# Folding w_in by even and odd frequencies in 64-column groups, with row sums made on GpSimd

## The chip, the cores and the metric

The kernel runs on one core of one Trainium2 chip. The metric is the time of one execution on the device in microseconds (us). TensorE (PE; its weight loads are PEld), VectorE (DVE), ScalarE (ACT), GpSimd (POOL) and SyncE (SP, which issues most DMAs) each work through their own queue of instructions in order and wait for one another by semaphores.

## The reference

```python
def _attn_ref(x):                      # x: (8, 3008, 256) float32
    X = np.fft.fft(x, axis=1)
    X = np.fft.fft(X, axis=2)
    return X.real.astype(np.float32)

def _moe_ref(x, w_in, w_out):          # x: (24064, 256), w_in (256, 2048), w_out (2048, 256)
    h = x @ w_in
    g = np.where(h > 0.0, h, np.exp(np.minimum(h, 0.0)) - 1.0)
    return (g @ w_out).astype(np.float32)
```

The weights are float64 in memory. The output of the first function, as 24064 rows of 256, is the input of the second.

## The kernel before

**The mathematics.** The transform over the 256 channels is linear and is followed at once by `w_in`, so the kernel never makes it for the data: it multiplies `w_in` by the cosines and sines of the channels instead. This is the *fold*: `Wc` (cosine part) and `Ws` (sine part), 128 x 2048 each. The transform over the sequence is done for the data, by matrices `MC00`, `MC01`, `MC10`, `MC11` (index: cosine or sine, even or odd frequency), on sums and differences of x: `fold_x` reads four pieces `xl0` to `xl3` of a batch and makes even sums `e0` to `e3` and odd differences `o0` to `o3` over channels c and 256 - c, then sums and differences of those (E0, E2, EO0 to EO3, O0, O2). Channel 128 goes a way of its own (`xe`, `rx`, `Rb`).

**Weights.** `w_in` and `w_out` come in eight chunks of 256 columns or rows each. Each is float64 and is turned into float32 by a class `Chunk`: `load` (SyncE's DMA into a *home*), `fields` (two VectorE operations, L212 and L218, on the words), `power` (three ScalarE operations, L366), `round` (GpSimd adds, `w<-raw,w`) and `scale` (VectorE, L255, then a GpSimd multiplication, `w<-w,pow`). The home of chunk c of `w_in` is the tile `WT0` to `WT3` for c = 0 to 3, a half of `Wc` for 4, and `WT0`, `WT1`, `WT2` for 5, 6, 7; homes are used again by later chunks. `fold_chunk(c)` then multiplies by the constants `CC` into PSUM (`H`), and `put_chunk(c)` copies the result to `Ws` and `Wc` on ScalarE.

**Steps.** The main loop has 376 steps of a period T = 4.8 (a unit close to a microsecond), eight for each tile of 256 sequence frequencies; a step treats 256 of the 2048 hidden columns. In each, TensorE multiplies `Wc` by the ring `Rr` (`mm_P`) and `Ws` by `Ir` (`mm_Q`), VectorE makes `E` (L728, from P, before Q may overwrite) and the two halves of the hidden layer (L738), ScalarE the exponentials, VectorE the ELU (L754), and TensorE multiplies by `w_out` into pA to pD. From the third tile on the second product is a Winograd form with seven blocks instead of eight, for which GpSimd makes sums of the activations (`G<-G`, four of 128 x 256 a step) and, once, of the weights: `sum_weights(i)`, four operations on 128 x 128, writes column i of the four tiles `WT0` to `WT3`, `WT2` first. The first 16 steps use the plain form; step pair 2c and 2c + 1 needs chunk c of `w_out`.

**The order.** There is no planner: `at(t, fn)` puts every piece of work at a time in units of the period, and the pieces are recorded sorted by t and kept in that order on each engine where they are pinned; DMAs, which are not, may be moved by the framework. `fold_chunk(c)` stands at `max(2c - 3, c % 3) * T + 4.7` for c > 1, just before the `mm_P` of a step. `sum_weights(i)` stands at `(11 + 0.7 i) T + 1.0`. `fold_x` of the next batch runs on GpSimd, in halves, spread over the steps.

**Channel 128.** At `12 T + 1.35` `ext_rows(1, gtt, 1)` writes two row pieces `rx` on GpSimd. From them SyncE copies to DRAM, and then 16 DMAs `load_ext` read channel 128 of all batches element by element into the same tile tag; `get_ext` brings it back by partition (`xs`), `fold_ext` on GpSimd adds (`xe`), and `dft_ext` on TensorE uses it in four column groups at `25 T + 4.75`. `dft_ext_0` (matmuls `MC,xd`) did the same for one batch earlier, in two groups with one column each.

Of the kernel before, what the change touches and what calls it, by code (L numbers as in the profile page):

```python
# [9 lines left out]
FP = mybir.dt.float32  # L10
# [5 lines left out]
ALU = mybir.AluOpType  # L16
# [39 lines left out]

def _chan_consts():

    c = np.arange(256)
    d = np.arange(129)  # L60
    cos = np.cos(2.0 * np.pi * ((c[:, None] * d[None, :]) % 256) / 256)
    d = np.arange(1, 128)
    sin = -np.sin(2.0 * np.pi * ((c[:, None] * d[None, :]) % 256) / 256)
    m = np.concatenate([cos[:, :128], sin, cos[:, 128:]], axis=1)
    return np.ascontiguousarray(
        m.reshape(2, 128, 256).transpose(1, 0, 2).reshape(128, 512)
    ).astype(np.float32)


# [9 lines left out]
def kernel(  # L79
# [7 lines left out]
    nc = tc.nc  # L87
# [19 lines left out]
    pin = tc.keep_in_program_order  # L107
# [52 lines left out]
        return L  # L160


    CC = cpool.tile([128, 512], FP, tag="CC")
    w2 = cpool.tile([128, NF * ND], FP, tag="w2")
    Wc = cpool.tile([128, NDFF], FP, tag="Wc")
    Ws = cpool.tile([128, NDFF], FP, tag="Ws")
# [7 lines left out]
    class Chunk:  # L174

        def __init__(self, src, dst, raw, tmp, shared):
            self.src, self.dst, self.home, self.tmp_tag = src, dst, raw, tmp
            self.shared = shared  # L180

        def load(self):
            dst = self.dst()
            if not wide:
                nc.sync.dma_start(out=dst, in_=self.src)
                return
            home = self.home
            if isinstance(home, tuple):
                tag, bufs, size = home
                home = spool.tile([128, size], FP, tag=tag, bufs=bufs, name="raw")  # L190
            words = home[:, 0:1024].bitcast(I32)
            self.raw = words.rearrange("p (n w) -> p n w", w=2)
            n = dst.shape[1]
            nc.sync.dma_start(
                out=words.rearrange("p (a b) -> p a b", a=n), in_=self.src.bitcast(I32)
            )
# [37 lines left out]
        def round(self):  # L234
# [11 lines left out]
                )  # L246
            )

        def scale(self):

            if not wide:
                return
            lo, hi, dst = self.parts()
            pin(
                nc.vector.scalar_tensor_tensor(  # L255
                    out=self.t, in0=hi, scalar=-(2**31), in1=self.t,
                    op0=ALU.bitwise_and, op1=ALU.bitwise_or,
                )
            )
            if self.shared:  # L260
                gtt(dst, dst, self.t.bitcast(FP), ALU.mult)
                return
            pin(
                nc.vector.scalar_tensor_tensor(
                    out=dst, in0=dst, scalar=2.0**-20,
                    in1=self.t.bitcast(FP), op0=ALU.mult, op1=ALU.mult,
                )
            )

    def w1_dst(c):  # L270
        q, half = divmod(c, 2)
        if q not in w1:
# [24 lines left out]
            IN_HOMES[c],  # L297
            IN_TMP[c],
            c > 0,
        )  # L300
        for c in range(8)
    ]
# [4 lines left out]
            OUT_HOMES[c],  # L307
            OUT_TMP[c],
            True,
        )  # L310
        for c in range(8)
    ]
# [39 lines left out]
    def mm(out_, lhsT, rhs, start, stop=True):  # L352
        pin(
            nc.tensor.matmul(  # L354
                out_, lhsT=lhsT, rhs=rhs, start=start, stop=stop, skip_group_check=True
            )
        )
# [4 lines left out]
    def gtt(o, a, b, op):  # L362
        pin(nc.gpsimd.tensor_tensor(out=o, in0=a, in1=b, op=op))  # L363
# [6 lines left out]

    def fold_chunk(c):

        q, half = divmod(c, 2)
        ps = folds[c] = bank("H")
        for n, part in enumerate((128, 0)):
            for h in range(2):
                mm(
                    ps[:, 256 * n : 256 * n + 256],
                    CC[:, h * 256 + part : h * 256 + part + 128],
                    w1[q][:, h, half * 256 : half * 256 + 256],  # L380
                    n == 0 and h == 0,
                    h == 1,
                )

    def put_chunk(c):
        cols = slice(c * 256, (c + 1) * 256)
# [43 lines left out]
        gtt(W[3], W[1], b21, ALU.add)  # L430


    OC = slice(0, 6 * 127)

    def fold_x(L, engine_of, pieces):

        ops = {}

        def op(key, o, a, b, f):
            tt = lambda o, a, b, f: pin(  # L440
                engine_of(key).tensor_tensor(out=o, in0=a, in1=b, op=f)
            )
            n = o.shape[1]
            cuts = [n * i // pieces for i in range(pieces + 1)]
            for i in range(pieces):
                c = slice(cuts[i], cuts[i + 1])
                ops[key, i] = lambda c=c: tt(o[:, c], a[:, c], b[:, c], f)

        E, O = [], []
        for j in range(4):  # L450
            e = spool.tile([128, 6 * 128], FP, tag=f"e{j}", bufs=1, name=f"e{j}")
            o = spool.tile([128, 6 * 127 + 1], FP, tag=f"o{j}", bufs=1, name=f"o{j}")
            ev = e.rearrange("p (m d) -> p m d", d=128)
            ov = o[:, OC].rearrange("p (m d) -> p m d", d=127)
            src = L[j].rearrange("p (m d) -> p m d", d=ND)
            if j in (1, 2):
                src = src[:, ::-1]
            lo, hi = src[:, :, 1:128], src[:, :, 255:128:-1]
            op(f"e{j}", ev[:, :, 1:128], lo, hi, ALU.add)
            ops[f"c{j}", 0] = lambda e=ev[:, :, 0:1], s=src[:, :, 0:1]: pin(  # L460
                engine_of("c").tensor_copy(out=e, in_=s)
            )
            op(f"o{j}", ov, lo, hi, ALU.subtract)
            E.append(e)
            O.append(o)
        ops["x1", 0] = lambda: act(L[1][0:1, 5 * ND :], L[0][0:1, 0:ND])
        for j in (1, 3):
            ops[f"z{j}", 0] = lambda o=O[j]: pin(
                nc.gpsimd.memset(o[:, 6 * 127 :], 0.0)
            )  # L470
        P = [o[:, OC] for o in O]
        op("E0", E[0], E[0], E[1], ALU.add)
        op("E2", E[2], E[2], E[3], ALU.add)
        op("EO0", E[1], E[0], E[2], ALU.add)
        op("EO1", E[3], E[0], E[2], ALU.subtract)
        op("O0", P[0], P[0], P[1], ALU.subtract)
        op("O2", P[2], P[2], P[3], ALU.subtract)
        op("EO2", P[1], P[0], P[2], ALU.subtract)
        op("EO3", P[3], P[0], P[2], ALU.add)
        return [E[1], E[3], O[1], O[3]], ops  # L480

    FOLDS = (
        "c0 e0 c3 e3 c2 e2 x1 c1 e1 E0 E2 EO0 o0 o3 o2 o1 z1 z3 O0 O2 EO2 EO1 EO3".split()
    )

    def fold_first(L):
# [45 lines left out]
    class Dft:  # L532
# [5 lines left out]
            self.ring = ring if ring is not None else (Ir if ri else Rr)  # L538

        def mms(self, par, ps):  # L540
            width = 1 if self.first else 127 if self.ri else 128
            dft_mms(ps, self.ri, self.kodd, par, self.stat, width)
            if par:
                self.pb = ps
            else:
                self.pa = ps
# [484 lines left out]
    def fold_now(keys):  # L1031
        for key in keys.split():
            ops[key, 0]()
# [9 lines left out]
    def at(t, fn):  # L1043
        events.append((t, len(events), fn))
# [17 lines left out]
        state["x_even"] = Dft(0, 0, 0, fold_first(L_first), ring=Rb, first=True)  # L1062

    at(-25.5, load_rest)
    at(-25.0, lambda: fold_now("z1 z3 c3 e3"))
    at(-24.9, w1_chunks[0].scale)
    at(-24.8, lambda: fold_now("o3 c2 e2 E2 o2 O2"))
    at(-24.5, begin_x_even)
    at(-24.4, lambda: fold_now("c0 e0 c1 e1 E0 EO0"))
    at(-20.7, lambda: load_mats(1, 1))  # L1070
    at(-20.6, w1_chunks[5].load)
    at(-20.5, w2_chunks[5].load)
# [25 lines left out]
    for chunk, k in (  # L1098
        (w2_chunks[0], 0),
        (w1_chunks[2], 1),  # L1100
        (w1_chunks[3], 2),
        (w2_chunks[1], 3),
        (w1_chunks[4], 4),
        (w2_chunks[2], 5),
        (w1_chunks[5], 6),
        (w2_chunks[3], 7),
        (w1_chunks[6], 8),
        (w2_chunks[4], 9),
        (w1_chunks[7], 10),
        (w2_chunks[5], 11),  # L1110
        (w2_chunks[6], 12),
        (w2_chunks[7], 14),
    ):
        t = k * T
        first = ((0.96, 0.96, 0.97, 1.9), (3.0, 3.05, 3.06, 4.22), (0.95, 0.96, 0.97, 4.2))
        dt = first[k] if k < 3 else (-0.5, 0.05, 0.06, 2.95)
        for d, fn in zip(dt, (chunk.fields, chunk.power, chunk.round, chunk.scale)):
            at(t + d, fn)
    for chunk, t in (
# [156 lines left out]
    at(27 * T + 1.0, lambda: ext_rows(0, vtt))  # L1276
    at(27 * T + 1.46, lambda: ext_side(3))
    at(28 * T + 1.35, lambda: ext_rows(1, gtt))
    fold_keys = [(k, p) for k in FOLDS for p in range(2 if k[0] not in "czx" else 1)]
    n_big = sum(k[0] not in "czx" for k, _ in fold_keys)  # L1280
    for b in range(1, NB):
        s0 = (b - 1) * steps_b
        l0 = s0 - 8 if b > 1 else 5.2
# [4 lines left out]
        for key in fold_keys:  # L1288
            at(
                int(f0 + n * (f1 - f0) / n_big) * T + 1.3,  # L1290
                lambda key=key: state["ops"][key](),
            )
            n += key[0][0] not in "czx"
        for n, (ri, kodd) in enumerate(((0, 0), (1, 0), (0, 1), (1, 1))):
            at_dft(
                s0 + (28, 34, 38, 42)[n], 2, b, ri, kodd,
# [56 lines left out]
```

## Time and profile before

| | |
|---|---|
| median of 9 runs | 1971.38 us (1970.89 to 1981.61) |
| the profiled execution, its own time | 1976.72 us |
| its span | 1974.9 us |
| busy: PE, DVE, POOL, ACT | 1959.3, 1274.5, 1334.6, 871.3 us |
| matmuls `H<-w,CC` (all eight folds) | 64 passes, 15.2 us |
| granted TensorE clock | 0.998 |

Times in the profile count from the start of the span. A group's row gives line, engine, operation, what is written and read, shape and count; in a timeline the first two numbers are the start and the length of a run of equal instructions, and the bracket tells how long the engine was idle before it and what released it. A float32 matmul shows as two passes. In the windows each engine has its busy time and its number of instructions, and after them come the granted clock, the share of the DMA engines and GB/s.

### The profile page before, as it was taken

Reading aid. Unit: us, or ns where it says so; the run is one execution under the profiler, and the core shown is the slowest. Engines: PE = TensorE matmul, PEld = TensorE weight load, DVE = VectorE, ACT = ScalarE, POOL = GpSimd, SP = SyncE. Lnnn points to the kernel's source line nnn. Section 1 sums busy time; section 2 is a strip of 40 time slices with the busy share of each in tenths; the row PEclk is TensorE's granted clock in tenths of the full one; section 3 lists DMA queues with packets and bytes.
Section 4 is the critical chain, followed back from the end, with each engine's and each line's share of the span. In section 5 each row is a group of like instructions: output and inputs, shape, how many; then the busy total and the mean of one; then the engine's idle time right before and its main releaser. Section 6 shows DMA issues by size and latency. Waiting matters only on the chain.

```text
span 1974.9 us, 26831 instructions
## 1 busy us (share of the span) xinstructions
PE 1959.3 (99%) x8900; PEld 1664.3 (84%) x8900; DVE 1274.5 (65%) x2325; ACT 871.3 (44%) x1667; POOL 1334.6 (68%) x1804
## 2 busy tenths in 40 slices
PE   9999999999999999999999999999999999999998
PEld 5887888888888888888888888888888888888887
DVE  8865566666667666666566665666556765666666
ACT  4654434444444444444344443444444444344443
POOL 3587758776577766777567775678657776455665
PEclk9999999999999999999999999999999999999999
DMA  9056200121001110021100211013010110100101
GB/s 366 22 21 54 74 13 19 33 59 24 12 19 43 46 29 12 18 57 34 26 18 13 66 25 26 11 19 89 7 21 12 20 22 14 16 12 12 22 9 24
DMA packets 255610, 71.08 MB, mean 36 GB/s; under 512 B 243998, under 2 KB 244786, under 8 KB 255088
## 3 DMA queue, kind: packets, MB, share of 16 engines
q1 hardware_dynamic: 250896, 56.52, 15.1%
q0 software_dynamic: 2400, 12.59, 1.9%
q8 instruction: 70, 1.15, 0.2%
q14 instruction: 68, 0.56, 0.1%
q10 hardware_dynamic: 2176, 0.26, 0.1%
HBM read 44.50 MB, written 24.80 MB: 35 GB/s over the span
## 4 chain that ended last, share of the span: by engine, by line
PE 92%; DMA 2%; SPq 2%; DVE 2%; POOL 1%; issue 1%; ACT 1%; POOLq 0%; DVEq 0%
PE H L354 37%; PE pD L354 16%; PE pC L354 16%; PE pB L354 16%; PE pA L354 8%; SPq L578 1%; DMA x<-in_x_dram 1%; DMA xl<-in_x_dram,ix 1%; DVE E L728 0%; SPq L595 0%; POOL G L363 0%; DVE v L360 0%; DVE G L754 0%; ACT G L366 0%; POOL w L363 0%
## 5 line engine op out<-in xcount | busy, mean ns | idle before, releaser
L363 POOL TENSOR_TENSOR G<-G 128x256 f32<-128x256 f32 x1440 | 1036.3, 729 | 565.9 <-DVE G L754 454.3
L728 DVE SCALAR_TENSOR_TENSOR E<-Rb,wex,H 128x256 f32<-128x256 f32 x752 | 327.9, 477 | 617.6 <-PE H L354 614.5
L366 ACT ACTIVATE G<-H 128x512 f32<-128x512 f32 x376 | 224.9, 598 | 951.5 <-DVE G L738 951.5
L354 PE MATMUL H<-Ir,Ws 128*128 128x256 f32 x1504 | 387.2, 380 | 2.1 <-DVE E L728 2.0
L354 PE MATMUL H<-Rr,Wc 128*128 128x256 f32 x1504 | 386.4, 379 | 0.0
L354 PE MATMUL pC<-G,WT 128*128 128x256 f32 x1440 | 369.5, 379 | 0.0
L354 PEld LDWEIGHTS H<-Rr,Wc 128*128 128x128 f32 x1504 | 285.1, 190 | 54.1 <-issue 2.6
L354 PEld LDWEIGHTS H<-Ir,Ws 128*128 128x128 f32 x1504 | 277.6, 189 | 51.0 <-DVE E L728 5.5
L354 PEld LDWEIGHTS pC<-G,WT 128*128 128x128 f32 x1440 | 273.6, 190 | 37.2
L738 DVE SCALAR_TENSOR_TENSOR G<-E,H 128x512 f32<-128x512 f32 x376 | 257.3, 685 | 37.1 <-PE H L354 1.6
L754 DVE SCALAR_TENSOR_TENSOR G<-G,H 128x512 f32<-128x512 f32 x376 | 256.0, 681 | 26.1 <-ACT G L366 26.0
L754 DVE SCALAR_TENSOR_TENSOR G<-M,G 128x512 f32<-128x512 f32 x376 | 257.3, 684 | 0.0
L366 ACT ACTIVATE G<-G 128x512 f32<-128x512 f32 x376 | 233.8, 622 | 0.0
L354 PE MATMUL pA<-G,w 128*128 128x256 f32 x784 | 229.4, 379 | 0.2 <-POOL w L363 0.2
L354 PE MATMUL pB<-G,w 128*128 128x256 f32 x784 | 229.3, 379 | 0.0
L354 PE MATMUL pD<-G,w 128*128 128x256 f32 x784 | 229.3, 379 | 0.0
L366 ACT ACTIVATE M<-G 128x512 f32<-128x512 f32 x376 | 224.6, 597 | 0.0
L366 ACT ACTIVATE M<-M 128x512 f32<-128x512 f32 x376 | 221.5, 589 | 0.1
L354 PE MATMUL pD<-G,WT 128*128 128x256 f32 x720 | 214.4, 379 | 1.6 <-DVE v L360 1.6
L354 PE MATMUL pB<-G,WT 128*128 128x256 f32 x720 | 214.3, 379 | 0.5 <-POOL G L363 0.5
L354 PEld LDWEIGHTS pA<-G,w 128*128 128x128 f32 x784 | 148.9, 190 | 20.8 <-POOL w L363 0.6
L354 PEld LDWEIGHTS pB<-G,w 128*128 128x128 f32 x784 | 149.0, 190 | 20.3
(132 smaller groups left out, 1389.2 us busy)
## 6 DMA issues: line engine op xcount, KB each, us to landing
out_dram<-ot SPq DMA_DIRECT2D x496, 32.0 KB
xl<-in_x_dram SPq DMA_DIRECT2D x16, 768.0 KB
out_dram<-ot SPq DMA_DIRECT2D x256, 2.0 KB
Rb<-r SPq DMA_DIRECT2D x10, 376.0 KB
raw<-in_moe_w_in_dram SPq DMA_DIRECT2D x7, 512.0 KB
MC<-dft_mats SPq DMA_DIRECT2D x3, 1131.0 KB
raw<-in_moe_w_out_dram SPq DMA_DIRECT2D x5, 512.0 KB
out_dram<-ot SPq DMA_DIRECT2D x64, 28.0 KB
```

Source lines behind the costliest of these rows:

```text
L354: nc.tensor.matmul(out_, lhsT=lhsT, rhs=rhs, start=start, stop=stop, skip_group_check=True)
L363: pin(nc.gpsimd.tensor_tensor(out=o, in0=a, in1=b, op=op))
L366: pin(nc.scalar.activation(out=o, in_=i, func=func, **kw))
L578: nc.sync.dma_start(out=t[:, s0:s1], in_=bass.AP(tensor=xt, offset=x.offset + row * ND + 128, ap=[[SEQ * ND, NB], [step * ND, s1 - s0], [1 ...
L728: nc.vector.scalar_tensor_tensor(out=S.E[:, c], in0=Rb[:, cols(i)], scalar=wex[:, f : f + 1], in1=S.H[:, c], op0=ALU.mult, op1=ALU.add,)
L738: nc.vector.scalar_tensor_tensor(out=two(S.G[:, 0:512])[:, :, ::-1], in0=two(S.E), scalar=2.0, in1=two(S.H), op0=ALU.mult, op1=ALU.subtract,)
L754: nc.vector.scalar_tensor_tensor(out=o, in0=e, scalar=-1.0, in1=h, op0=ALU.add, op1=ALU.max)
```

## The change

The sequence fold of channels stays, but channel frequencies are kept in the order odd, then even (`fold_x` writes `e` and `o` as two runs of 64, reading x at every second element, 128 wide for `o` too, where it was 127). With even and odd frequencies apart, the fold of `w_in` needs for each only the sum or only the difference of the rows c and c + 128 of `w_in`. Chunks 1 to 7 get these from GpSimd (`pair`, two operations of 128 x 256 after `scale`, into the chunk's home), and `fold_chunk` makes four matmuls with 64 columns of `CC`, two in either half of the columns of the array, where it made four with 128. Chunk 0 has no sums: it makes eight matmuls of 64 columns over both halves of the rows. The constants shrink from 512 to 384 columns. `fields`, `power` and `round` of chunks 2 and 3 of `w_in` and 1 of `w_out` get other times, and the copy `c` of each piece now follows its `e`.

```diff
-    m = np.concatenate([cos[:, :128], sin, cos[:, 128:]], axis=1)
+    even, odd = np.arange(0, 129, 2), np.arange(1, 128, 2)
+    ... # seven blocks of 128 x 64 columns: cosines and sines of even and of odd frequencies
-    CC = cpool.tile([128, 512], FP, tag="CC")
+    CC = cpool.tile([128, 384], FP, tag="CC")
...
         def load(self):
             dst = self.dst()
+            home = self.home
+            if isinstance(home, tuple) and (wide or self.pairs):
+                tag, bufs, size = home
+                home = spool.tile([128, size], FP, tag=tag, bufs=bufs, name="raw")
+            self.ab = home[:, 0:512]
...
+        def pair(self):
+            dst = self.dst()
+            gtt(self.ab[:, 0:256], dst[:, 0], dst[:, 1], ALU.add)
+            gtt(self.ab[:, 256:512], dst[:, 0], dst[:, 1], ALU.subtract)
+
         def scale(self):
+            self.multiply()        # what scale was before
+            if self.pairs:         # chunks 1 to 7 of w_in
+                self.pair()
...
     def fold_chunk(c):
-        q, half = divmod(c, 2)
         ps = folds[c] = bank("H")
-        for n, part in enumerate((128, 0)):
-            for h in range(2):
-                mm(
-                    ps[:, 256 * n : 256 * n + 256],
-                    CC[:, h * 256 + part : h * 256 + part + 128],
-                    w1[q][:, h, half * 256 : half * 256 + 256],
-                    n == 0 and h == 0,
-                    h == 1,
-                )
+        chunk = w1_chunks[c]
+        dst = chunk.dst()
+        for n in range(2):
+            cols = slice(256 * n, 256 * n + 256)
+            for h in range(1 if chunk.pairs else 2):
+                for half in range(2):
+                    odd = n == half
+                    block = 2 * odd + half + 2 * (odd and h)
+                    mm(
+                        ps[64 * half : 64 * half + 64, cols],
+                        CC[:, 64 * block : 64 * block + 64],
+                        chunk.ab[:, 256 * odd : 256 * odd + 256]
+                        if chunk.pairs
+                        else dst[:, h],
+                        n == 0 and h == 0,
+                        h == 1 or chunk.pairs,
+                    )
...
-            o = spool.tile([128, 6 * 127 + 1], FP, tag=f"o{j}", bufs=1, name=f"o{j}")
-            ev = e.rearrange("p (m d) -> p m d", d=128)
-            ov = o[:, OC].rearrange("p (m d) -> p m d", d=127)
+            o = spool.tile([128, 6 * 128], FP, tag=f"o{j}", bufs=1, name=f"o{j}")
+            ev, ov = (
+                t.rearrange("p (m o d) -> p m o d", o=2, d=64) for t in (e, o)
+            )
...
-            lo, hi = src[:, :, 1:128], src[:, :, 255:128:-1]
-            op(f"e{j}", ev[:, :, 1:128], lo, hi, ALU.add)
+            lo, hi = (
+                t.rearrange("p m (d o) -> p m o d", o=2)
+                for t in (src[:, :, 1:129], src[:, :, 255:127:-1])
+            )
+            op(f"e{j}", ev, lo[:, :, ::-1], hi[:, :, ::-1], ALU.add)
...
-        "c0 e0 c3 e3 c2 e2 x1 c1 e1 E0 E2 EO0 o0 o3 o2 o1 z1 z3 O0 O2 EO2 EO1 EO3".split()
+        "e0 c0 e3 c3 e2 c2 x1 e1 c1 E0 E2 EO0 o0 o3 o2 o1 O0 O2 EO2 EO1 EO3".split()
...
-        first = ((0.96, 0.96, 0.97, 1.9), (3.0, 3.05, 3.06, 4.22), (0.95, 0.96, 0.97, 4.2))
-        dt = first[k] if k < 3 else (-0.5, 0.05, 0.06, 2.95)
+        first = (
+            (0.96, 0.96, 0.97, 1.9),
+            (2.1, 2.9, 2.91, 4.22),
+            (2.95, 2.96, 2.97, 4.2),
+            (0.95, 0.96, 0.97, 4.2),
+        )
+        dt = first[k] if k < 4 else (-0.5, 0.05, 0.06, 2.95)
```

The row k of `first` belongs to w_out chunk 0, w_in chunks 2 and 3 and w_out chunk 1, in this order; its four numbers are the times of `fields`, `power`, `round` and `scale` within step k. In the order that results, the raw words of chunk 2 also stand ahead of `MC10` in SyncE's queue, where they stood behind it.

More of the change, by code (lines that the diff above doesn't have):

```diff
@@ L57, in _chan_consts, with block @@
 def _chan_consts():
[L59 to L63, printed above, removed]
-    m = np.concatenate([cos[:, :128], sin, cos[:, 128:]], axis=1)
-    return np.ascontiguousarray(
-        m.reshape(2, 128, 256).transpose(1, 0, 2).reshape(128, 512)
+    c = np.arange(128)[:, None]
+    def block(fn, d):
+        return fn(2.0 * np.pi * ((c * d[None, :]) % 256) / 256)
+    even, odd = np.arange(0, 129, 2), np.arange(1, 128, 2)
+    return np.concatenate(
+        [
+            block(np.cos, np.roll(even[:64], -1)),
+            -block(np.sin, even[1:64]),
+            block(np.cos, even[64:]),
+            -block(np.sin, odd),
+            block(np.cos, odd),
+            block(np.sin, odd),
+            -block(np.cos, odd),
+        ],
+        axis=1,
     ).astype(np.float32)
@@ L174, with __init__ @@
     class Chunk:
-        def __init__(self, src, dst, raw, tmp, shared):
+        def __init__(self, src, dst, raw, tmp, shared, pairs):
             self.src, self.dst, self.home, self.tmp_tag = src, dst, raw, tmp
-            self.shared = shared
+            self.shared, self.pairs = shared, pairs
         def load(self):
             dst = self.dst()
+            home = self.home
[3 more added lines that the diff above has]
+            self.ab = home[:, 0:512]
             if not wide:
@@ L186, in load @@
                 return
[L187 to L190, printed above, removed]
             words = home[:, 0:1024].bitcast(I32)
@@ L247, in round, with multiply @@
             )
+        def pair(self):
+            dst = self.dst()
+            gtt(self.ab[:, 0:256], dst[:, 0], dst[:, 1], ALU.add)
+            gtt(self.ab[:, 256:512], dst[:, 0], dst[:, 1], ALU.subtract)
         def scale(self):
+            self.multiply()
+            if self.pairs:
+                self.pair()
+        def multiply(self):
             if not wide:
@@ L299 @@
             c > 0,
+            c > 0,
         )
@@ L309 @@
             True,
+            False,
         )
@@ L430, in sum_weights @@
         gtt(W[3], W[1], b21, ALU.add)
-    OC = slice(0, 6 * 127)
     def fold_x(L, engine_of, pieces):
@@ L457, in fold_x @@
                 src = src[:, ::-1]
-            lo, hi = src[:, :, 1:128], src[:, :, 255:128:-1]
-            op(f"e{j}", ev[:, :, 1:128], lo, hi, ALU.add)
-            ops[f"c{j}", 0] = lambda e=ev[:, :, 0:1], s=src[:, :, 0:1]: pin(
+            lo, hi = (
[3 more added lines that the diff above has]
+            op(f"e{j}", ev, lo[:, :, ::-1], hi[:, :, ::-1], ALU.add)
+            ops[f"c{j}", 0] = lambda e=ev[:, :, 0, 63:64], s=src[:, :, 0:1]: pin(
                 engine_of("c").tensor_copy(out=e, in_=s)
@@ L466, in fold_x @@
         ops["x1", 0] = lambda: act(L[1][0:1, 5 * ND :], L[0][0:1, 0:ND])
[L467 to L471, printed above, removed]
         op("E0", E[0], E[0], E[1], ALU.add)
@@ L475, in fold_x @@
         op("EO1", E[3], E[0], E[2], ALU.subtract)
[L476 to L479, printed above, removed]
+        op("O0", O[0], O[0], O[1], ALU.subtract)
+        op("O2", O[2], O[2], O[3], ALU.subtract)
+        op("EO2", O[1], O[0], O[2], ALU.subtract)
+        op("EO3", O[3], O[0], O[2], ALU.add)
         return [E[1], E[3], O[1], O[3]], ops
     FOLDS = (
-        "c0 e0 c3 e3 c2 e2 x1 c1 e1 E0 E2 EO0 o0 o3 o2 o1 z1 z3 O0 O2 EO2 EO1 EO3".split()
+        "e0 c0 e3 c3 e2 c2 x1 e1 c1 E0 E2 EO0 o0 o3 o2 o1 O0 O2 EO2 EO1 EO3".split()
     )
@@ L540, in mms @@
         def mms(self, par, ps):
-            width = 1 if self.first else 127 if self.ri else 128
-            dft_mms(ps, self.ri, self.kodd, par, self.stat, width)
+            dft_mms(ps, self.ri, self.kodd, par, self.stat, 1 if self.first else 128)
             if par:
@@ L1064 @@
     at(-25.5, load_rest)
-    at(-25.0, lambda: fold_now("z1 z3 c3 e3"))
+    at(-25.0, lambda: fold_now("e3 c3"))
     at(-24.9, w1_chunks[0].scale)
-    at(-24.8, lambda: fold_now("o3 c2 e2 E2 o2 O2"))
+    at(-24.8, lambda: fold_now("o3 e2 c2 E2 o2 O2"))
     at(-24.5, begin_x_even)
-    at(-24.4, lambda: fold_now("c0 e0 c1 e1 E0 EO0"))
+    at(-24.4, lambda: fold_now("e0 c0 e1 c1 E0 EO0"))
     at(-20.7, lambda: load_mats(1, 1))
@@ L1278 @@
     at(28 * T + 1.35, lambda: ext_rows(1, gtt))
-    fold_keys = [(k, p) for k in FOLDS for p in range(2 if k[0] not in "czx" else 1)]
-    n_big = sum(k[0] not in "czx" for k, _ in fold_keys)
+    fold_keys = [(k, p) for k in FOLDS for p in range(2 if k[0] not in "cx" else 1)]
+    n_big = sum(k[0] not in "cx" for k, _ in fold_keys)
     for b in range(1, NB):
@@ L1292 @@
             )
-            n += key[0][0] not in "czx"
+            n += key[0][0] not in "cx"
         for n, (ri, kodd) in enumerate(((0, 0), (1, 0), (0, 1), (1, 1))):
```

## The prediction

> **What bounds the kernel now.** I read the busy shares first, then the same shares by stage.
>
> ```profile
> PE 1959.3 (99%) x8900; PEld 1664.3 (84%) x8900; DVE 1274.5 (65%) x2325; ACT 871.3 (44%) x1667; POOL 1334.6 (68%) x1804
> ...
> 44.00:116.00 72.00, 70.31 (x321) 58.29 (x320) 56.76 (x89) 45.41 (x89) 42.60 (x40) 1.00 0.12 40
> 116.00:181.00 65.00, 62.20 (x290) 54.29 (x290) 40.35 (x72) 29.63 (x57) 53.25 (x79) 0.99 0.78 13
> 181.00:400.00 219.00, 218.49 (x997) 185.07 (x995) 138.31 (x257) 94.41 (x181) 155.88 (x212) 0.99 0.19 45
> ```
>
> TensorE (third number) idles 0.5 us from 181 to 400 and 2.8 us from 116 to 181. That idle time is one wait, so I followed the chain of waits through it.
>
> ```profile
> 111.50 1.30 POOL w L363
> 112.80 1.40 POOL e L441
> 114.19 1.88 POOL rx L363 x2
> 116.09 1.16 DMA r<-rx
> ...
> 176.60 2.10 DMA xs<-xe_dr
> ...
> 180.54 0.31 POOL xe L363
> ...
> 180.89 4.67 PE H L354 x28
> ```
>
> `ext_rows` on GpSimd ends at 116.07. SyncE then issues the single-channel loads, which run on the DMA engines until 178.7, and the matmuls on `xe` start at 180.89, with TensorE idle since 178.1. This stretch of 64.8 us holds no step of TensorE, so time that TensorE saves earlier only lengthens its wait at 180.89. The end moves by as much as the end of `rx` moves, if TensorE is not later than that. The question is when GpSimd reaches `rx`.
>
> **One fold.** Durations come from this profiled execution (1976.72 us, span 1974.9); its median is 1971.38, and I carry the difference over unchanged.
>
> ```profile
> 98.04 1.89 PE L354 MATMUL pB<-G,w 128*128 128x256 f32 x8
> 99.86 2.06 PE L354 MATMUL H<-MC,xd 128*1 128x376 f32 x12
> 101.86 1.13 PE L354 MATMUL H<-Rr,Wc 128*128 128x256 f32 x4
> ...
> 107.14 1.89 PE L354 MATMUL H<-w,CC 128*128 128x256 f32 x8
> 108.87 1.03 PE L354 MATMUL H<-Rr,Wc 128*128 128x256 f32 x4
> 109.73 1.89 PE L354 MATMUL pA<-G,w 128*128 128x256 f32 x8
> ```
>
> Each matmul is two passes; eight passes of 256 take 108.87 - 107.14 = 1.73, or 0.216 each. The middle row of the first three shows two column groups: 12 passes of 376, which would take 12 x 0.316 = 3.8 one after another (0.316 from the six-pass rows of the same width), stand 2.00 before the next row, so the two groups run side by side in 6 x 0.316 = 1.90. Entering and leaving cost 0.09 (98.04 + 8 x 0.216 = 99.77, not 99.86), 0.10, and 0.10 in the next row's first pass (102.82 - 101.86 = 0.96, not 0.86). A paired fold is again eight passes, in two groups: 4 x 0.216 + 0.29 + 0.03 for its wider weight loads = 1.18, a saving of 0.55. Bounds: without side-by-side work 1.73 + 0.3 = 2.0; the `MC,xe` row, four groups, reached half of the ideal (24 passes in 3.5 us).
>
> [...]
>
> Chunk 0 keeps the same work in 16 half passes: 1.73 + 0.3, ending about 15.7, under the wait for `xe` on VectorE that ends at 16.28.
>
> **How far ahead TensorE is when fold 7 starts (107.14 before).** I take the events in order; plus is earlier.
> - Start: each copy c now follows its e and holds up the next sum: VectorE's E2 by 0.12, then EO0 by 0.36 in all, on which pA (20.20) waits: -0.36. The constants' load is 64 KB smaller, which frees no wait there. The raw words of chunk 2 (512 KB) now pass the matrices 1,0 on SyncE: at about 400 GB/s, 1.3 us later, 23.1 instead of 21.8, still before their first reader at 23.9.
> - Chunk 1: GpSimd's multiplication ends 29.32 + 0.36; two sums of 128x256, four of which take 3.03 (0.76 each), end at 31.2. The fold would start at 31.0 and waits: lead -0.07 after it.
> - 40.72, wait for E on VectorE: its predecessor L255 is held by GpSimd's operation until 40.1, E ends at 40.9: -0.23. Fold 2: +0.32.
> - 49.36, 1.6 us of waiting plus 0.1 of refilling: E stood behind two operations of w_out chunk 1 (46.70 and 48.11). They now come after it, and TensorE arrives when E is done: +2.05. Fold 3: +2.60. Then w_out chunk 1 itself is late: its second VectorE operation is held by sums 3 until 48.1, ScalarE's three (0.6 each) end at 49.2, GpSimd adds until 50.55, L255 is held until 51.1, the multiplication (1.3) ends at 52.4, 0.4 after TensorE comes: +2.15.
> - Folds 4 and 5: +3.25. The waits at 89.69 (0.28) go: +3.5. Fold 6: +4.05. At 95.35 TensorE waits for GpSimd's w_out chunk 4; in GpSimd's queue two e (to 85.4), the multiplication of chunk 6 (86.65), now sums 6 (88.2), the addition (89.5), copy and e (90.9) and the multiplication stand in a row, so it is ready at 92.2, and the lead drops to +3.1.
>
> So fold 7 starts near 104.0. At nothing I cost pairs 3, 4, 5 and 7, which end 1.5 to 6 us before their folds, and the loads that now wait for a fold before they may reuse a home: chunk 6 (29.8 to 32.4, with the x loads of batch 1 behind it on SyncE, not read before 83), chunk 7, w_out 3, and w_out 4, which goes from 72.3 to 78.5 and lands some 3 us later, 1 us before VectorE reads it. If that cover went, its delay would fall on the same wait at 95.35.
>
> **The new wait.**
>
> ```profile
> 103.12 1.29 POOL L363 TENSOR_TENSOR w<-raw,w 128x512 f32<-128x512 f32 x1 [2.27 <-ACT w L366]
> 104.38 0.45 POOL L363 TENSOR_TENSOR WT<-w 128x128 f32<-128x128 f32 x1
> ...
> 108.09 1.26 POOL L363 TENSOR_TENSOR w<-w,pow 128x512 f32<-128x512 f32 x1
> ```
>
> The sums of chunk 7 lie in WT2, and the first `sum_weights` writes WT2. It may now start only when fold 7 has been read out of it, and the rest of GpSimd's queue stands behind it: four WT operations, a copy, an e, the last multiplication of w_out chunk 5, four more WT, w, e, rx. Fold 7's last pass ends 1.15 after its start, so GpSimd goes on at 105.2 rather than at 104.38 - 3.1 = 101.3. Then 1.8 + 0.35 + 1.05 + 1.26 = 4.5: chunk 5 is ready at 109.7. TensorE wants it at 106.1 (before, 109.73 with 0.4 to spare) and waits 3.6 us: its whole lead is gone. GpSimd continues: 1.8 + 1.3 + 1.0 + 1.9 = 6.0, rx ends at 115.7; with the durations that the same rows had beside a busy VectorE (WT 2.2, e 1.4), 116.6. Middle 116.2 against 116.07: +0.1 us.
>
> From 181 on nothing gains or loses. The sums of x read every second element; `w<-raw,w` reads its low words so, in 1.30 against 1.27 for `w<-w,pow`. [...]
>
> **Rivals.**
> - The saving reaches the end. If fold 7's release came as early as its neighbours' work, rx would move with the lead of 3.1 + 0.5: 1967.8. For it: all earlier waits show that GpSimd and VectorE follow TensorE. Against: the WT2 order in the program. Chance 0.10.
> - The change doesn't do what it says: the 64-column groups do not overlap, and a fold costs 0.3 more instead of 0.55 less. Over six folds the lead at fold 7 falls from 3.1 to about -0.3 (the later waits shrink with it), fold 7 is 0.85 longer, rx comes 4 us later: 1975.4. For: the `MC,xe` row. Against: the `MC,xd` row. Chance 0.08.
> - Slower: GpSimd slowed by reading at stride two. Per step of 4.75 us it has 3.03 of Winograd sums, and in many steps one x sum of 1.00. From 1.72 us per x sum the step overflows; at 2.0 each of 16 sums per batch loses 0.28, 4.5 us a batch, up to 31 us over seven batches: 2003. Against: 1.30 beside 1.27. Chance 0.06.
>
> **How the numbers follow.** 1971.38 + 0.1 = 1971.5, chance 0.76; its own bounds are 1969.5 (a lead of 4.5 at fold 7, short durations) and 1974 (lead 1.5, long ones). The range adds the second rival's price and half a microsecond below: 1969.0 to 1975.4. A difference of 0.2%, 3.9 us, is about what a measurement of this kernel can tell from no change. The first rival's 3.6 stays mostly inside it (0.03 outside, and 0.02 from an `rx` that moves more than the lead); half of the second, the third and a little of the forecast lie above. Faster 0.05, same 0.82, slower 0.13.
>
> **What would show it.** Fold 7 in about 1.2 us and near 104; the first WT operation idle before it, released by PE; pA near 109.7 idle for 3 to 4 us, released by POOL w; no wait at 49.36; rx ending within 1 us of 116.1; the wait at 180.9 still there. If rx ends before 113 or after 119, or the x sums take over 1.7 us, the prediction is wrong.

## The result, and the profile after

The changed kernel takes 1977.49 us (median of 14 runs, 1976.43 to 1983.7); the kernel before takes 1971.64 (43 runs). The ratio is 1.0029, 95% interval 1.002 to 1.0037: slower by 5.9 us, where 1971.5 was forecast. The profiled execution took 1983.35 us, its span 1981.6; it lies 5.9 us above the median of its kernel, and the section on the experiments says where.

The busy shares and the three windows answer to those of before (busy PE is the third number of a window):

```profile
PE 1958.8 (99%) x8908; PEld 1657.2 (84%) x8908; DVE 1275.3 (64%) x2325; ACT 869.0 (44%) x1667; POOL 1362.0 (69%) x1802
...
44.00:116.00 72.00, 64.99 (x301) 49.13 (x301) 54.88 (x85) 44.03 (x87) 47.16 (x47) 0.98 0.12 39
116.00:181.00 65.00, 65.00 (x302) 57.00 (x302) 39.02 (x71) 30.48 (x58) 55.70 (x78) 1.00 0.84 10
181.00:400.00 219.00, 214.74 (x977) 181.32 (x976) 136.33 (x254) 92.46 (x178) 154.43 (x206) 0.99 0.19 42
```

TensorE is busy for as long as before (1958.8 against 1959.3 us) in a span that is 6.7 us longer: its idle time grew from 15.6 to 22.8 us. Two stretches hold it: TensorE idles 7.0 us from 44 to 116 (before 1.7), and 4.3 us from 181 to 400 (before 0.5; here the wait for `xe` falls into this window). The timelines of TensorE and GpSimd around fold 7:

```profile
106.90 1.08 PE L380 MATMUL H<-raw,CC 128*64 128x256 f32 x8
107.92 1.13 PE L380 MATMUL H<-Rr,Wc 128*128 128x256 f32 x4
112.94 3.64 PE L380 MATMUL pA<-G,w 128*128 128x256 f32 x8 [3.90 <-POOL w L389]
116.42 1.03 PE L380 MATMUL H<-Ir,Ws 128*128 128x256 f32 x4
```

```profile
102.54 1.29 POOL L389 TENSOR_TENSOR w<-raw,w 128x512 f32<-128x512 f32 x1 [1.77 <-ACT w L392]
108.14 0.46 POOL L389 TENSOR_TENSOR WT<-w 128x128 f32<-128x128 f32 x1 [4.31 <-PE H L380]
...
111.18 1.71 POOL L389 TENSOR_TENSOR w<-w,pow 128x512 f32<-128x512 f32 x1
...
117.00 1.91 POOL L389 TENSOR_TENSOR rx<-bs 1x376 f32<-1x376 f32 x2
```

The predicted wait is there. GpSimd has nothing to do from 103.8 on, the first weight sum starts only after fold 7 (released by PE), and TensorE then waits 3.90 us for the multiplication of w_out chunk 5 (4.06 where I take gaps from start to start at the pace of the passes, as I do from here on). What the prediction did not have stands in the third row of TensorE: `pA` takes 116.42 - 112.94 = 3.48 us to the next row, where the same eight passes took 1.73 before. The windows of just these passes give the granted clock (third number from the end), here 0.52:

```profile
112.94:116.42 3.48, 3.48 (x9) 2.82 (x9) 0.00 (x0) 0.00 (x0) 3.40 (x6) 0.52 0.02 5
186.74:189.91 3.17, 3.17 (x25) 1.06 (x25) 0.00 (x0) 0.00 (x0) 3.01 (x6) 0.70 0.87 226
```

The second row is the passes on `xe`, where the clock was 0.70. With each of these two rows goes a stretch of 3.41 us at half speed: the granted clock was 0.50 from 112.90 to 116.31, behind the gap of 4.06 us, and from 187.99 to 191.40, behind the wait for `xe`, and 1.00 between the two. The gap that it takes is another matter, and comes last.

The chain of waits of the changed kernel runs through the same places as before:

```profile
108.14 0.47 POOL WT L389
...
111.22 1.68 POOL w L389
112.94 3.64 PE pA L380 x8
...
169.02 11.78 DMA x<-in_x_dram
180.88 1.61 DMA xe_dr<-x
182.50 2.06 DMA xs<-xe_dr
...
186.74 5.02 PE H L380 x28
```

The matmuls on `xe` start at 186.74 (before 180.89), and TensorE was idle in front of them in both of these profiles. So two routes meet there: the loads that follow `rx`, and TensorE itself, which arrived at 182.90 (before at 177.93), 5.0 us later than before. In the table below "TensorE at xe" is this arrival, the end of the last pass before `xe`, and the wait follows in brackets.

### The profile page after: what moved, and what is told of

Same layout as the page of the kernel before. It is cut to its first block, busy times and chain, and to the rows that moved or that the text cites. A ratio compares the mean times of both kernels' runs of the same rounds, so it can differ in the third digit from the quotient of the medians.

```text
span 1981.6 us, 26860 instructions
## 1 busy us (share of the span) xinstructions
PE 1958.8 (99%) x8908; PEld 1657.2 (84%) x8908; DVE 1275.3 (64%) x2325; ACT 869.0 (44%) x1667; POOL 1362.0 (69%) x1802
## 4 chain that ended last, share of the span: by engine, by line
PE 92%; DVE 2%; SPq 2%; DMA 2%; issue 1%; POOL 1%; ACT 0%; POOLq 0%; DVEq 0%
PE H L380 37%; PE pD L380 16%; PE pB L380 16%; PE pC L380 15%; PE pA L380 8%; SPq L609 2%; DMA x<-in_x_dram 1%; DVE E L759 0%; DMA wex<-wx 0%; POOL w L389 0%; DVE pow L279 0%; SPq L626 0%; POOL xl L157 0%; DVE G L785 0%; DVE v L386 0%
```

## The experiments

All but the second profile of the kernel before were timed (5 to 12 runs each) beside runs of the kernel before on the same chip, whose medians were 1971.66, 1971.71 and 1971.67. Columns three to five are from the one profile of each. The time from the start of the matmuls on `xe` to the end of the span lies between 1792.8 and 1793.4 us in every profile without a half clock there, and time and span differ by 1.8, so a time of 1971.6 belongs to a start at 177 and one of 1977.5 to a start near 183. The profile of the changed kernel shows what put it above its median: it waited 3.85 us at `xe` and then ran at half clock (1794.9 from there to the end instead of 1793), together 5.7 of the 5.9 us.

| kernel | median us | ratio, 95% interval | fold 7 starts | rx ends | TensorE at xe (wait) |
|---|---|---|---|---|---|
| before | 1971.64 | | 107.14 | 116.07 | 177.93 (2.96) |
| before, second profile | 1973.37, one run | | 106.35 | 115.30 | 177.15 (1.65) |
| changed | 1977.49 | 1.0029 (1.002 to 1.0037) | 106.90 | 118.91 | 182.90 (3.85) |
| weight sums later | 1973.71 | 1.0008 (0.9997 to 1.0018) | 105.48 | 114.08 | 177.82 (0) |
| chunk 7 without sums | 1973.74 | 1.0012 (1.0000 to 1.0025) | 107.09 | 116.27 | 178.14 (0) |
| no sums | 1975.15 | 1.0014 (1.0000 to 1.0028) | 106.45 | 115.62 | 177.50 (0) |
| row 127 of chunk 0 on TensorE | 1978.07 | 1.003 (1.0019 to 1.004) | 106.12 | 118.12 | 182.15 (0) |
| only chunk 7 with sums | 1978.74 | 1.0036 (1.0022 to 1.005) | 106.62 | 118.61 | 182.66 (2.88) |
| spare matmuls | 1977.56 | 1.0032 (1.002 to 1.0044) | 107.20 | 119.20 | 182.75 (0) |
| weight sums in between | 1976.06 | 1.0019 (1.001 to 1.0028) | 106.40 | 114.99 | 178.69 (0.85) |
| all four | 1972.47 | 1.0004 (0.9995 to 1.0013) | 103.83 | 108.00 | 178.55 (0) |
| sums to chunk 5 | 1970.62 | 0.9987 (0.9978 to 0.9997) | 106.18 | 110.56 | 177.23 (0) |
| before, rx early | 1971.10 | 0.9995 (0.9984 to 1.0006) | 105.77 | 109.85 | 176.56 (0) |
| own buffer for chunk 7 | 1971.26 | 1.0004 (0.9993 to 1.0014) | 105.34 | 113.92 | 175.78 (0.2) |

The theory was that the wait of the first weight sum for fold 7 is the whole loss, and that it acts on TensorE directly. Its rivals were a later start (chunk 0's longer fold), GpSimd's added work, and the loads behind `rx` as the only route.

**The wait moved behind.** The first edit of the changed kernel:

```diff
-        at((11 + 0.7 * i) * T + 1.0, lambda i=i: sum_weights(i))
+        at((12.4 + 0.6 * i) * T + 1.0, lambda i=i: sum_weights(i))
```

> The changed kernel with the eight sum_weights 1.4 periods later and 0.6 apart, so that the first stands behind rx in GpSimd's queue; all else as changed. Theory (the wait for fold 7 before WT2 may be written holds GpSimd, and so w_out chunk 5 and rx): no idle time of TensorE at pA after fold 7 (4.1 us in the changed kernel), rx ends near 114.9 (118.9 changed, 116.1 before), xe near 180 to 183, time 1970.4 if the single-channel loads take the 64.8 us from rx to xe of before, up to 1973.4 if they keep the 67.8 of the changed kernel. Rival (the lead lost in the start-up decides): still about 1976. Rival (slower sums of x from 181 on): still 1976 to 1977.

1973.71: 3.8 us of the 5.9 are back, with fold 7's successors in line (timeline of TensorE, this kernel):

```profile
105.48 1.08 PE L380 MATMUL H<-raw,CC 128*64 128x256 f32 x8
106.49 1.13 PE L380 MATMUL H<-Rr,Wc 128*128 128x256 f32 x4
107.46 0.81 PE L380 MATMUL pA<-G,w 128*128 128x256 f32 x3
...
141.45 0.70 PE L380 MATMUL pB<-G,WT 128*128 128x256 f32 x2 [1.88 <-POOL G L389]
```

The last row is a new wait: with the weight sums pushed back, GpSimd is late with the first sums of activations, at the first product that reads `WT`. The experiment moved part of the loss instead of removing it.

**No sums for chunk 7**, and **none for any chunk**: `c > 0` of the pairs becomes `0 < c < 7`, or `False`. Folds without sums make eight matmuls over both halves of the rows.

> The changed kernel with chunk 7 folded without sums, as chunk 0 is (eight matmuls of 64 columns, no pair), so that its home WT2 is free early; sum_weights as it was. Theory: the same wait goes in another way; fold 7 is 0.9 us longer, no idle time at pA after it, rx ends near 115.8, time 1971 to 1974. Rivals: 1977 plus up to 0.9.

> The changed kernel with no sums at all: every chunk folded as chunk 0 is, 2.0 us each instead of 1.0. Nothing waits for fold 7 and GpSimd has 14 operations less. Theory: fold 7 starts near 107.6 and rx ends near 116.8 although TensorE works 7 us more on folds, time 1972.4, faster than the changed kernel. Rival (TensorE's own work decides): 7 us slower than the changed kernel, 1984. Rival (the strided sums of x cost the time): as the changed kernel, 1977.

1973.74 and 1975.15. Both lose the idle time after fold 7. By the medians, a kernel whose folds 1 to 7 are each 0.9 us longer than folds from sums (1.88 against 1.02) is still 2.3 us faster than the changed one, so the fold's length did not make the change slow. The expected 1972.4 fits the profile of this kernel (1972.72) but not its median, and the cause of the 2.4 us between the two is open.

**Chunk 0's last row without DMA.** In the profile after, TensorE waited 1.30 us at 30.58 for `wex`, which comes through DRAM from chunk 0's fold.

```diff
-    at(-13.05, lambda: spread_last_row(0))
+    at(-12.95, lambda: turn_last_row(0))
+    at(-12.0, lambda: put_last_row(0))
```

> The changed kernel with the last row of chunk 0 turned by two small matmuls and a ScalarE copy, as for chunk 1, instead of the two DMAs through GpSimd's queue. If the 1.3 us that TensorE waits at 30.6 for VectorE, which waits for wex, are what the lead lacks: that wait goes, fold 7 starts up to 1.2 us earlier, near 105.7, rx up to 1.2 earlier, time 1976.3 at best. If the waits at 91 and 95 for GpSimd eat it: fold 7 and rx move by less than 0.4, 1977. In both the wait after fold 7 stays, about 4 us.

1978.07, no gain, although its profile shows no wait at 30. The same wait was 0.21 us in the own-buffer kernel, which has chunk 0 as the changed one has it, and 0.96 in the second profile of before. It changes from execution to execution in both kernels, and a later start is refuted as the cause: fold 7 came 0.8 us earlier here, and the time did not fall.

**The wait alone.** Sums for chunk 7 only (`c == 7`):

> Sums only for chunk 7; chunks 1 to 6 are folded in eight matmuls of 64 columns over both halves of the rows (about 0.7 us longer each than a fold from sums). Only the wait of the first weight sum for fold 7 is left of what the sums bring. If that wait alone makes the change slow: fold 7 at 106 to 107, TensorE idle about 4 us behind it, rx ending 12 us after fold 7's start, time 1977 to 1978.5, as the changed kernel's 1977.5. If instead the extra work of GpSimd for all seven chunks is what costs: no more than 1974 to 1975, as without any sums (1975.15).

1978.74: with one pair of sums in place of seven the loss is complete, idle time (4.06 us again) and all. GpSimd's added work for chunks 1 to 6 is not what costs.

**A buffer of its own.** The order of all work stays; only the address changes:

```diff
             self.ab = home[:, 0:512]
+            if self is w1_chunks[7]:
+                self.ab = spool.tile([128, 512], FP, tag="ab", bufs=1, name="ab")
```

> The changed kernel with a buffer of its own for the sums of chunk 7, instead of the home that the first weight sum writes; the order of all work is the same. If the wait for fold 7 is the whole loss: the first weight sum right behind w<-raw,w, no idle time after fold 7 and no half clock, TensorE at xe near 177, 1971.5 to 1972.5. If the added work of GpSimd (14 sums, longer x sums) costs beyond it: 1973.5 to 1975.

1971.26, as before (ratio 1.0004, 0.9993 to 1.0014). GpSimd's and TensorE's timelines of this kernel:

```profile
100.98 1.29 POOL L391 TENSOR_TENSOR w<-raw,w 128x512 f32<-128x512 f32 x1 [1.76 <-ACT w L394]
102.24 0.45 POOL L391 TENSOR_TENSOR WT<-w 128x128 f32<-128x128 f32 x1
...
112.00 1.92 POOL L391 TENSOR_TENSOR rx<-bs 1x376 f32<-1x376 f32 x2
```

```profile
105.34 1.08 PE L382 MATMUL H<-ab,CC 128*64 128x256 f32 x8
106.35 1.13 PE L382 MATMUL H<-Rr,Wc 128*128 128x256 f32 x4
107.47 1.99 PE L382 MATMUL pA<-G,w 128*128 128x256 f32 x8
```

The first weight sum follows its neighbour at once, 3.1 us before fold 7, and `pA` runs at full speed (1.83 us to its next row, at 109.30). This isolates the cause: a wait that comes only from a home used again, not from the data, costs all of the 5.9 us. The new layout of `e` and `o` and all 14 sums are in this kernel too, so neither made the change slow.

**Which route sets the end.** In the kernel before, `rx` alone was moved up:

```diff
-    at(12 * T + 1.35, lambda: ext_rows(1, gtt, 1))
+    at(11 * T + 3.0, lambda: ext_rows(1, gtt, 1))
```

> The kernel before with rx right behind the last multiplication of w_out chunk 5 (11 steps plus 3.0 instead of 12 plus 1.35), so 4 to 5 us earlier, and nothing else. If the end moves as rx moves, as the prediction had it: 1968 to 1969, until TensorE's own arrival binds. If in most executions TensorE arrives at xe later than the loads: 1971.7, no change, only fewer runs at 1974 and above.

`rx` ends at 109.85, 6.2 us earlier than in the first profile of before and 5.5 than in the second, and the median moves by 0.6 us (ratio 0.9995, 0.9984 to 1.0006). TensorE's rows of this kernel at `xe`, then those of the kernel before in its second profile:

```profile
176.13 0.59 PE L354 MATMUL pD<-G,w 128*128 128x256 f32 x2
176.66 2.09 PE L354 MATMUL H<-MC,xe 128*8 128x377 f32 x24
178.68 1.13 PE L354 MATMUL H<-Rr,Wc 128*128 128x256 f32 x4
```

```profile
176.72 0.59 PE L354 MATMUL pD<-G,w 128*128 128x256 f32 x2
178.80 2.31 PE L354 MATMUL H<-MC,xe 128*8 128x377 f32 x24 [1.49 <-POOL xe L363]
```

> The kernel before unchanged, for a second profile. If its first profile (time 1976.7, TensorE 2.96 us idle before xe) was one of the executions in which the single-channel loads took long: here a span near 1970, TensorE at xe near 177 without idle time, the last of the loads back well before. If the wait for xe belongs to every execution: again 2 to 3 us of it.

The second profile of before has its wait too, but a shorter one, and its single time, 1973.37, is above the median by 1.7 us, about the length of that wait. By the sum above, a median of 1971.6 belongs to a start at 177 and leaves no room for a wait. No profile of the kernel before is of such an execution; the one with `rx` early is (arrival 176.56, no wait, 1971.49), and with the loads out of the way it gained only 0.6. The loads are the bound of some executions, TensorE's own arrival that of the usual one.

**The half clock alone.** 14 spare matmuls in the idle time after fold 7:

```diff
+    def keep_clock():
+        spare = bank("M")
+        for _ in range(14):
+            mm(spare, zero, zero[:, 0:1].to_broadcast([128, 512]), True)
+    at(12 * T + 0.86, keep_clock)
```

> The changed kernel with 14 spare bf16 matmuls on a zero tile (0.21 us each, 3 us together) in TensorE's idle time after fold 7; nothing waits for them. Clock theory: the 8 passes after the idle stand 0.216 apart instead of 0.427, TensorE reaches the matmuls on xe 1.9 us earlier (181 in place of 182.9); if TensorE's arrival there sets the end, 1975.6. If the chain from rx through the single-channel loads sets it (rx ends at the same 118 to 119), TensorE waits longer at xe and the time stays within 0.7 us of 1977.5. If the half clock comes from something other than the idle, the passes stay at 0.427.

1977.56, unchanged, and this one stays inconclusive about the price. The spare matmuls did not start in the idle time's first part but at 111.50, after waiting 2.17 us themselves, and lasted until 114.55, while `pA` could have begun near 113.2 (6.0 after fold 7's start, as in the changed kernel). `pA` then took the normal 1.72 us to its next row (114.55 to 116.27): a gap of 2.3 us and busy time behind it left the clock at 1.00. So the slow passes do come from the idle time, but of the 1.75 us that they no longer cost, the late spare matmuls took 1.3.

**Room for both.** Weight sums between the two places (`12.1 + 0.55 * i`); then the same with `rx` early, chunk 0's row on TensorE, and the first three x sums of batch 1 at steps 11 to 13:

> The weight sums start at 12.1 steps plus 1.0 and follow every 0.55 steps: behind fold 7 and rx in GpSimd's order, and done where the changed kernel has them done. With the sums at 12.4 plus 0.6 each (1973.7) TensorE waited 2.05 us at 141.45, at the first product that reads them. If that wait is what was left of the loss: no wait behind fold 7 and none at 141, TensorE at xe near 175.8, and 1971 to 1972.5, as before, held up only where the chain from rx (ending near 114) is later than TensorE. If the rest of the loss is elsewhere (start-up, steady state): 1973.5 again.

> The weight sums as in the run between, the sums rx right behind the last multiplication of w_out chunk 5 (11 steps plus 3.0 instead of 12 plus 1.35; near 107.5 instead of 114), chunk 0's row 127 turned to a column on TensorE instead of by DMA, and the first three x sums of batch 1 moved from steps 8 to 9 to steps 11 to 13, out of the stretch where GpSimd was late with the sums of chunk 6 and w_out chunk 4 (waits of 0.56 and 1.95 us on TensorE). If the two routes to the matmuls on xe (TensorE's own arrival and the chain from rx) are all that sets the end: TensorE there at 172.5 to 175, xe not later, time 1967 to 1970.5, under both kernels. If a floor lies elsewhere: 1971.5.

1976.06 and 1972.47. Both lost the wait behind fold 7 and got another one at `pA` near 130, of 1.6 and 2.5 us, released by a multiplication of GpSimd. The work that was moved in is the likely cause, but no run tests that. The second had fold 7 at 103.83, the earliest of all, and still reached `xe` at 178.55: from fold 7 to `xe` it took 74.7 us, the own-buffer kernel 70.4, and 2.5 of the 4.3 between them are this wait.

**Sums to chunk 5**, with `rx` early and chunk 0's row on TensorE, weight sums and x sums where the change has them:

```diff
             c > 0,
-            c > 0,
+            0 < c < 6,
```

> Sums for chunks 1 to 5 only (6 and 7 from both halves of the rows, 0.7 us longer each), weight sums where the changed kernel has them, rx right behind the last multiplication of w_out chunk 5, chunk 0's row 127 turned on TensorE. Nothing of chunks 6 and 7 then holds GpSimd between 86 and 107: the waits of 0.56 and 1.95 us at w_out chunk 4 should go, with the half clock that followed the second in some runs, no wait for fold 7, none at 130 or 141. If TensorE's own waits set the end: TensorE at xe near 174 and 1968 to 1970, faster than both kernels. If the x sums and multiplications of GpSimd alone keep TensorE waiting there: 1972 to 1974, as with sums for 1 to 6 (1973.7).

1970.62, ratio 0.9987 (0.9978 to 0.9997), the fastest kernel of the study, by 1.0 us against the one before, of which `rx` early alone gives 0.6 (1971.10). The expectation was 1968 to 1970. The waits of 0.56 and 1.95 us at w_out chunk 4 are gone, but a new one of 0.7 us stands at 88.8, and those of 1.3 and 1.1 us at 41.7 and 54.1 remain.

## Why the prediction was wrong

**What held.** A fold from sums takes 107.92 - 106.90 = 1.02 us, with 0.09 to enter and 0.10 in the next row's first pass: 1.2, predicted 1.18. The four rounds of weight loads show next to no time of their own: the 1.02 us are 0.16 more than four rounds of 0.216, where the `MC,xd` row of before took 0.10 more than six of 0.316 (2.00). The wait at 49.36 went (0.07 left). The new wait has its predicted place, releaser and size (3.90, predicted 3.6), and `rx` ends 12.0 us after fold 7's start (predicted 11.7 to 12.6). From `xe` on nothing changed, though the x sums on GpSimd became longer than assumed. The sign "the wait at 180.9 still there" came true by luck: the profiled execution was again one far above its median.

**First failed step: "time that TensorE saves earlier only lengthens its wait at 180.89", and the end moves as `rx` moves.** The 2.96 us of waiting in the profile of before belong to executions with slow loads. Moving `rx` by 6 us moved the median by 0.6. The prediction named the condition itself ("if TensorE is not later than that") and took it as met. In the usual execution TensorE has no slack at `xe`, so each microsecond that it loses after fold 7 is a microsecond of the end. The warning stood in the times: the profiled execution lay 5.3 us above the median, and I carried that over as a constant instead of asking which wait it was. With the end tied to `rx`, the measured 2.84 us of the next step would have made 1971.38 + 2.84 = 1974.2; most of the 3.3 us from there to 1977.49 are this step's.

**Second failed step: the lead of 3.1 us at fold 7.** It was 0.24, and the forecast of `rx` needed all of it: 0.1 + 2.86 = 3.0, measured 118.91 - 116.07 = 2.84. Start of each fold, before minus after:

| fold | 1 | 2 | 3 | 4 | 5 | 6 | 7 |
|---|---|---|---|---|---|---|---|
| predicted | -0.62 | -0.23 | 2.05 | 2.15 | 2.70 | 3.50 | 3.10 |
| measured | -1.07 | -0.92 | 1.14 | 0.45 | 0.96 | 1.30 | 0.24 |

The predicted row is worked out from its steps. What is missing grows from fold to fold by 0.45, 0.24, 0.22, 0.79, 0.04, 0.46 and 0.66. A first part is the start-up of the profiled execution. The largest single one is w_out chunk 1: predicted ready at 52.4, it was ready at 53.9, and TensorE waited 1.1 us at 54.00. The sums of chunk 3 were to end at 48.1 and ended at 50.2: the addition of their chunk waited for ScalarE until 45.14, and the multiplication ahead of them, from 46.55, took 1.88 us (the same row before: 1.85). The last two parts, 1.12 together, are GpSimd's queue at chunk 6. TensorE's wait for w_out chunk 4 before, then its waits for the sums of chunk 6 and for w_out chunk 4 after:

```profile
95.35 1.99 PE L354 MATMUL pA<-G,w 128*128 128x256 f32 x8 [0.21 <-POOL w L363]
```

```profile
91.09 1.08 PE L380 MATMUL H<-raw,CC 128*64 128x256 f32 x8 [0.39 <-POOL raw L389]
...
95.02 1.99 PE L380 MATMUL pA<-G,w 128*128 128x256 f32 x8 [1.78 <-POOL w L389]
```

The prediction had no wait for the sums of chunk 6, and w_out chunk 4 ready at 92.2; it was ready at 94.96. GpSimd's queue follows TensorE, so most of these 2.8 us is lead that was missing already (the two `e` ahead were to end at 85.4 and ended at 87.73); the sums took 1.99 us for two instead of 0.76 each, 0.5 more.

At 40.72 the predicted hold was there and its size was not right: L255 (now L279) stands beside GpSimd's addition until 40.17, as predicted (40.1), but then needs another 0.55 us, which the prediction left out: 1.66 us in all, where it took 0.69 before. The holds of the prediction come from rows of the kernel before, as L212: 0.42 us at 36.76, with GpSimd idle, and 1.49 at 46.70, most of it beside GpSimd's multiplication from 46.06 to 47.91. VectorE in the kernel before, then after, then that addition:

```profile
39.19 0.69 DVE L255 SCALAR_TENSOR_TENSOR pow<-raw,pow 128x512 int32<-128x512 int32 x1 [0.52 <-ACT pow L366]
39.80 0.86 DVE L728 SCALAR_TENSOR_TENSOR E<-Rb,wex,H 128x256 f32<-128x256 f32 x2
```

```profile
39.06 1.66 DVE L279 SCALAR_TENSOR_TENSOR pow<-raw,pow 128x512 int32<-128x512 int32 x1
40.64 0.86 DVE L759 SCALAR_TENSOR_TENSOR E<-Rb,wex,H 128x256 f32<-128x256 f32 x2
```

```profile
38.87 1.30 POOL L389 TENSOR_TENSOR w<-raw,w 128x512 f32<-128x512 f32 x1 [2.13 <-ACT w L392]
```

So even without the WT2 wait the folds bring little. In the own-buffer kernel the five waits at 40.01, 46.6, 52.43, 89.52 and 93.45 add up to 4.9 us, those of the second profile of before between the same folds, 1 and 7, to 2.5. Six folds at 0.53 save 3.2 there, the waits take 2.4 of it, and 0.8 is left: from fold 1 to fold 7 the two profiles differ by (106.35 - 30.15) - (105.34 - 29.95) = 0.81.

**A term that was missing: the clock.** The prediction put no price on the passes behind the wait. After the gap of 4.06 us `pA` cost 3.48 - 1.73 = 1.75 us more. From the start of fold 7 to `xe`, TensorE took 76.0 us against 70.8: the 5.2 are the wait (4.06) and the half clock (1.75), less what fold 7 and the row behind it save (1.98 instead of 2.59: 0.61). With the lead of 0.24 against it that makes 5.0 of the 5.9 between the medians. The other 0.9 I can't assign; the two profiles of before differ by 0.8 in TensorE's arrival.

**The rivals.** The folds do overlap, so the second rival fell; but the row that spoke for it was misread. `MC,xe` took 3.5 us before because the clock was down, not because four groups cost double. Its window in the kernel before, and the same 24 passes in the kernel with `rx` early:

```profile
180.89:184.41 3.52, 3.52 (x24) 1.39 (x24) 0.00 (x0) 0.00 (x0) 3.36 (x6) 0.59 0.88 247
```

```profile
176.66:178.68 2.02, 2.02 (x26) 0.57 (x25) 0.75 (x2) 0.59 (x2) 1.86 (x3) 1.00 0.87 333
```

At full clock 24 passes in four groups take 2.02 us, close to the ideal 24 x 0.316 / 4 = 1.9. The third rival fell too: x sums of `e` and `o` take 1.19 and 1.18 us on average against 1.02 and 1.00, far from the 1.72 from which a step overflows. The first rival asked for an early release of GpSimd. The own buffer gives that, and the time is 1971.26, not 1967.8, since other waits take the saving.

## What to carry to other kernels

When results are put into a buffer that something else will use next, ask which engine must finish reading before that next writer may start, and what stands behind the writer in its queue: here one address, not the added work, cost all of the loss, and a buffer of 2 KB per partition took it away. Before a wait in a profile is counted as slack, compare that execution's time with the median: a wait that is in the profile but not in the usual run hides nothing. And price an idle gap of TensorE with the passes behind it: here `pA` cost 1.75 us more behind the gap of 4.06 (granted clock 0.52), and the passes on `xe` 1.50 more in the kernel before (3.52 us at 0.59 against 2.02 at 1.00).

## What the runs showed of the hardware

The length of the gap alone does not tell in these runs whether half clock follows. After a wait at the same place, `pA` behind w_out chunk 4, the granted clock differs between two kernels, chunk 7 without sums (gap 1.96 us), then own buffer (gap 1.95):

```profile
93.52:96.74 3.22, 3.22 (x9) 2.57 (x10) 1.75 (x2) 0.00 (x0) 3.22 (x3) 0.56 0.02 0
```

```profile
93.45:95.28 1.83, 1.83 (x8) 1.63 (x9) 1.75 (x2) 0.00 (x0) 1.83 (x2) 1.00 0.08 1
```

The eight passes took 3.22 us in the first and 1.83 in the second. Other gaps, with the granted clock of what followed:

| gap, us | kernel and place | granted clock behind it |
|---|---|---|
| 4.06 | changed, `pA` after fold 7 | 0.52 (112.94 to 116.42) |
| 4.06 | only chunk 7 with sums, `pA` after fold 7 | 0.63 (112.50 to 116.20) |
| 3.85 | changed, `xe` | 0.70 (186.74 to 189.91) |
| 2.96 | before, `xe` | 0.59 (180.89 to 184.41) |
| 2.3 | spare matmuls, ahead of them | 1.00 (111.50 to 120.00) |
| 1.65 | before, second profile, `xe` | 1.00 (178.80 to 181.05) |

With the first, third and fourth of them goes a stretch at 0.50, 3.41 us long each time (in the kernel before from 180.35 to 183.76). What decides between the gaps of 1.95 and 1.96 us was not shown.

The 16 single-channel loads also vary more than expected: from the first load to the issue of the last `xs`, 48.1 us in the kernel without sums for chunk 7 (118.19 to 166.31) and 61.7 in the changed one (120.83 to 182.50). What makes them vary stays open.
